# A gated recurrence with a rational MLP on one core: three more accumulating DMAs, two copies moved from ScalarE to VectorE, and all 861 steps in a new order

## The chip, the cores and the metric

The kernel runs on one core of one Trainium2 chip. The metric is device time in microseconds of one execution. Of the kernel before, three runs are shown: 217.76, 218.05 and 218.08 us, median 218.05.

## What is computed

The reference, cut to what matters: a recurrence with a gate per key channel, whose output feeds an MLP with a rational activation.

```
f = 1 / (1 + exp(-f_logit))                        # (4, 8, 768, 48): batch, heads, steps, channels
for t in range(S):
    state = f[t][:, None] * state + outer(k[t], v[t])
    y[t]  = q[t] @ state
x  = y, heads side by side                          # (3072, 384)
h  = x @ w_in                                       # (3072, 2048)
P  = a0 + a1*h + a2*h^2 + a3*h^3
Q  = 1 + |b0|*|h| + |b1|*h^2
out = (P / (Q + 1e-6)) @ w_out                      # (3072, 384)
```

## The kernel before

The work is cut into 12 units of 256 tokens: unit n is chunk n // 4 of batch n % 4, so a unit needs the state that unit n - 4 left. Within a unit a partition holds two neighbouring tokens, and the hidden layer of 2048 lies as 16 blocks (`m`) of 128; the elementwise work on it goes by halves (`0 8`, `8 16`) or quarters (`0 4` and so on).

Nothing orders the steps but a string of 861 steps written out by hand, `ORDER` (lines 19 to 104). Each step issues its instructions on one engine, each engine takes its own in the order of the string, and semaphores hold a step until what it reads is there and what it overwrites has been read. `@s` names the one of four PSUM slots that a step opens; opening it waits for the readers of what lay there. `s` sends a copy to ScalarE (ACT), no letter to VectorE (DVE). The steps that matter here, with their lines in the kernel before:

- `ld` (L200): loads of f, k, q over SP's queue, of v over POOL's; three buffers each, so that a load waits for the last reader of an older one. `wi` (L206) and `wo` (L212) load the two weights over POOL's queue.
- Attention. ACT: `ef` (L278) and `ls` (L283) make log(1 + exp(-f)) of a unit; PE: `cs` (L293) sums it along the tokens; ACT: `A` (L309) takes exp of plus and minus the sum; DVE: `xa` (L315) multiplies A with q (`x` = 0) and k (`x` = 1); PE: `T` (L327) transposes; `Te` (L337 on ACT, L339 on DVE) copies the transposed tile out of PSUM; PE: `sc` (L352); DVE: `mk` (L360) masks; PE: `yi`, `yb` (L374) build y, `kv`, `si` (L421 to L432) the new state; ACT: `ae` (L445), DVE: `st` (L449) close the state; ACT: `ye` (L439) copies y out. POOL: `vm` (L367) packs parts of v.
- MLP. PE: `h` (L458; `ha` and `hb`, L482, for the first block); `hy` (L488) copies h out of PSUM, in quarters; DVE: `sq` (L492) h^2, or ACT: `sa` (L496); DVE: `ab` (L500) |h|.
- The denominator: its sum of h^2 and |h| is made in one of three ways: by PE, `u` (L508), read by `ln` (L513); by DVE, `zv` (L518); or by an accumulating DMA of POOL's queue, `zd` (L522), which adds h2 onto z in SBUF. `lz` (L526) takes the log of z, `ex` (L530) the exp of minus that.
- The numerator: DVE: `p1` (L534), `pm` (L548), `p2` (L539); then the sum of both parts is made by DVE, `tv` (L556), or by an accumulating DMA, `ta` (L552), which adds hy onto g; DVE: `gm` (L560) multiplies by the reciprocal.
- PE: `o` (L570) multiplies with w_out; `oe` (L577) copies out; `so` (L583) stores, on SP's queue but for the last, which is on ACT's. `dz` (L302) are matmuls whose result nobody reads.

A half of `tv` and a half of `ta` write the same bytes; so do halves of `zv` and `zd`. POOL takes its `vm`, its loads and its accumulating DMAs in one line: whichever waits holds up those behind it. The same holds for SP's loads and stores.

Of the kernel before, what the change touches and what calls it, by code (L numbers as in the profile page):

```python
# [13 lines left out]
ALU = mybir.AluOpType  # L14
# [5 lines left out]
ld 0 f 2 4; cz 0; ab_ b a; cu 0; cz 1; ld 0 f 0 2; ld 1 f; ci; cu 1; ld 0 v; ld 0 k 0 2; ld 0 k 2 4; fa  # L20
ld 0 q 2 4; ef 0 2 4; ls 0 2 4; cm; ef 0 0 2; dz 9 @2; cs 0 2 4 @2; fr; cz 3; ls 0 0 2; ld 0 q 0 2; ab_ a s
ld 1 k; dz 5 @3; cs 0 0 2 @3; ef 1; ld 1 q; ls 1; vm 0 1; A 0 1 0 2; wi 12 16 >ls.1; dz 4 @0; cs 1 @0
A 0 1 2 4; xa 0 1 0 2; A 0 0 2 4; wi 8 12; cz 2; A 0 0 0 2; xa 0 1 2 4; dz 3 @1; kv 0 @2; wi 4 8
xa 0 0 0 2; si 0 0; ae 0; dz 1 @1; T 0 0 2 @1; wi 0 4; xa 0 0 2 4; st 0 0; Te 0 0 2 s; T 0 2 4 @3; A 1 1
ld 1 v; Te 0 2 4; A 1 0; vm 0 0; sc 0 0 @1; si 0 1; mk 0 0; sc 0 1 @3; mk 0 1; ld 2 f >mk.0.1; ld 2 k
ld 3 f; yi 0 1 @0; yb 0 0 2; ye 0 0 1 s; xa 1 1; dz 2 @1; yb 0 2 4; ye 0 1 3 s; st 0 1; dz 1 @3
ha 0 12 16 @3; hb 0 12 16; xa 1 0; fb; hy 0 12 16; h 0 8 12 @1; sq 0 12 16; T 1 @3; hy 0 8 12; ab 0 12 16
u 0 12 16 @2; Te 1 s; sq 0 8 12; h 0 4 8 @1; p1 0 8 16; ln 0 12 16; ld 4 f; ab 0 8 12; pm 0 8 16
u 0 8 12 @2; hy 0 4 8; p2 0 8 16; ln 0 8 12; dz 1 @3; sc 1 1 @1; sc 1 0 @3; sq 0 4 8; h 0 0 4 @0; ef 2
ab 0 4 8; mk 1 1; ld 2 q; ls 2; u 0 4 8 @2; hy 0 0 4; mk 1 0; cs 2 @1; ld 3 q; vm 1 1; ln 0 4 8; vm 1 0  # L30
ld 2 v; kv 1 @0; p1 0 0 8; si 1 0; sq 0 0 4; A 2 1; ld 4 q; ld 3 v; ae 1; yb 1 2 4 @2; ab 0 0 4; A 2 0
yb 1 0 2; st 1 0; ld 4 v; xa 2 1; ef 3; yi 1 1; ld 3 k; u 0 0 4 @1; ye 1 s; tv 0 8 16; wo 8 12; si 1 1
ex 0 8 16; h 1 12 16 @2; p2 0 0 8; pm 0 0 8; h 1 0 4 @3; ld 4 k; ln 0 0 4; st 1 1; hy 1 12 16; tv 0 0 8
hy 1 0 4; h 1 4 8 @1; vm 2 1; xa 2 0; wo 12 16; h 1 8 12 @2; hy 1 4 8; ld 5 f; gm 0 8 16; vm 3 1; vm 2 0
wo 0 4; ls 3; T 2 @3; ab 1 0 8; hy 1 8 12; kv 2 @1; sq 1 0 8; Te 2 s; cs 3 @0; vm 3 0; wo 4 8; sq 1 8 16
ld 5 q; si 2 0; ae 2; A 3 0; sc 2 0 @2; sc 2 1 @3; A 3 1; ab 1 8 16; ex 0 0 8; st 2 0; u 1 4 8 @0; mk 2 1
si 2 1; mk 2 0; u 1 0 4 @3; ef 4; ln 1 4 8; st 2 1; yi 2 1 @2; yb 2 0 2; yb 2 2 4; p1 1 0 16; ld 5 k
ln 1 0 4; u 1 8 12 @0; vm 4 0; ld 5 v; ye 2 s; gm 0 0 8; u 1 12 16 @3; ln 1 8 12; xa 3 1; h 2 4 8 @1
ln 1 12 16; pm 1 8 16; ex 1 0 8; h 2 8 12 @3; xa 3 0; h 2 0 4 @0; pm 1 0 8; hy 2 8 12; ld 6 f; hy 2 4 8
p2 1 0 16; kv 3 @2; si 3 0; ae 3; hy 2 0 4; h 2 12 16 @1; st 3 0; tv 1 0 8; sa 2 8 12; T 3 @0; hy 2 12 16  # L40
ab 2 0 8; si 3 1; sq 2 0 8; Te 3 s; ld 6 k; sa 2 12 16; ab 2 8 16; sc 3 1 @3; u 2 4 8 @0; st 3 1; ls 4
# [72 lines left out]
def kernel(  # L114
# [12 lines left out]
    nc = tc.nc  # L127
    B, H, S, D = q.shape
    C = 128
# [4 lines left out]
    KD = DM // P  # L134
# [332 lines left out]
    def fl(t, m0, m1):  # L467
        return t[:, m0:m1, :].rearrange("p m t -> p (m t)")
# [17 lines left out]
    def hy(n, m0, m1):  # L486
        s = unit(n)
        nc.scalar.copy(fl(big(s, "hy", "hy", 3), m0, m1), fl(s["hp", m0], 0, m1 - m0))  # L488
# [140 lines left out]
```

## Time and profile before

| | before |
|---|---|
| median of three runs | 218.05 us |
| span of the profiled execution | 216.3 us |
| instructions in it | 7159 |
| PE, DVE, ACT, POOL busy | 203.2, 202.7, 200.8, 81.6 us |
| moved by DMA | 42.13 MB |

The profiled execution's own time is known by its span alone, from its first to its last instruction; the median stands 1.75 us above that span, and what is worked out below is worked out for the span and carried over with that difference kept. Back to back, instructions of one engine overlap a little in these records, so the cost of one in a busy stretch is the distance from its start to the start of the next, which is less than its duration.

### The profile page before, as it was taken

To read this page: it belongs to the slowest core of one execution; us is meant where nothing else is said; L and a number is where in the kernel's file an instruction comes from. 1 tells how busy PE (TensorE), PEld (TensorE's weight loads), DVE (VectorE), ACT (ScalarE), POOL (GpSimd) and SP (SyncE) were. 2 spreads that over 40 slices of the span, in tenths; PEclk is the share of its full clock that TensorE was granted. 3 is DMA by queue.
4 is the path that set the end of the run, shared out by engine and by line. 5 is a ranking of instruction groups with operands and counts; after the bars stand their busy time and mean duration, and the time that the engine had idled before them with its cause. 6 is when DMAs were issued, how large, how long until landed. Compare 5 with 4: busy or idle time off the path is not lost.

```text
span 216.3 us, 7159 instructions
## 1 busy us (share of the span) xinstructions
PE 203.2 (94%) x3166; PEld 140.1 (65%) x3166; DVE 202.7 (94%) x246; ACT 200.8 (93%) x211; POOL 81.6 (38%) x91
## 2 busy tenths in 40 slices
PE   6989989699799999999999999999999999999993
PEld 2457658468377657658758658668668678676551
DVE  3588999999999999999999999999999999999991
ACT  4746899999999999999999999999999999999991
POOL 5250247120157803014954205954232516433300
PEclk9999999999999999999999999999999999999999
DMA  5999999999598999958999997999889793999863
GB/s 132 248 226 194 243 212 226 207 221 250 136 246 143 231 237 271 149 101 195 197 232 216 211 251 179 173 234 222 160 159 228 142 162 70 170 194 188 154 234 145
DMA packets 60910, 42.13 MB, mean 195 GB/s; under 512 B 51152, under 2 KB 54992, under 8 KB 60880
## 3 DMA queue, kind: packets, MB, share of 16 engines
q0 software_dynamic: 21232, 22.81, 66.0%
q1 hardware_dynamic: 39360, 18.68, 33.7%
q8 instruction: 24, 0.39, 0.7%
q10 hardware_dynamic: 288, 0.20, 0.3%
q14 instruction: 6, 0.05, 0.1%
HBM read 25.17 MB, written 4.72 MB: 138 GB/s over the span
## 4 chain that ended last, share of the span: by engine, by line
ACT 42%; DVE 21%; PE 18%; DMA 8%; issue 6%; POOL 3%; POOLq 0%; ACTq 0%; DVEq 0%
ACT qi L530 11%; ACT hy L488 10%; PE op L570 9%; ACT lq L526 8%; DMA fn<-in_f_logit_dram 4%; DMA z<-h 4%; PE warm L302 3%; DVE gall L548 3%; ACT A L309 3%; DVE scm L360 3%; DVE qkp L315 3%; PE hp L458 2%; DVE gall L560 2%; DVE gall L556 2%; ACT qkT L337 2%
## 5 line engine op out<-in xcount | busy, mean ns | idle before, releaser
L570 PE MATMUL op<-w_out_sb,gall 128*128 128x384 bf16 x384 | 70.1, 326 | 0.4 <-ACT hy L488 0.4
L458 PE MATMUL hp<-xT,w_in_sb 128*128 128x256 bf16 x564 | 65.3, 272 | 1.3 <-ACT xT L439 1.1
L458 PEld LDWEIGHTS <-w_in_sb 128*128 128x128 bf16 x564 | 55.0, 98 | 11.0 <-issue 2.8
L570 PEld LDWEIGHTS <-gall 128*128 128x128 bf16 x384 | 35.5, 98 | 23.6 <-DVE gall L560 0.9
L488 ACT CAST hy<-hp 128x1024 bf16<-128x1024 f32 x48 | 47.4, 1073 | 1.7 <-PE hp L482 1.2
L530 ACT ACTIVATE qi<-lq 128x2048 bf16<-128x2048 f32 (+1 forms) x26 | 46.9, 1845 | 0.0
L367 POOL COPY vmp<-vn 128x128 bf16<-128x128 bf16 x24 | 33.7, 1417 | 32.1 <-DMA vn<-in_v_dram 18.9
L526 ACT ACTIVATE lq<-z 128x2048 f32<-128x2048 bf16 (+1 forms) x20 | 36.9, 1846 | 0.6 <-DMA z<-h 0.5
L552 POOL DMA_DIRECT2D gall<-hy x17 | 14.8, 926 | 50.7 <-ACT A L309 11.5
L522 POOL DMA_DIRECT2D z<-h x18 | 17.3, 1065 | 36.3 <-issue 10.5
L560 DVE TENSOR_TENSOR gall<-gall,qi 128x2048 bf16<-128x2048 bf16 (+1 forms) x26 | 29.6, 1143 | 0.3 <-ACT qi L530 0.2
L548 DVE TENSOR_TENSOR gall<-gall,h 128x2048 bf16<-128x2048 bf16 (+1 forms) x26 | 29.4, 1138 | 0.0
L492 DVE TENSOR_TENSOR h<-hy 128x2048 bf16<-128x2048 bf16 (+1 forms) x26 | 27.3, 1059 | 1.5 <-ACT hy L488 1.4
L360 DVE TENSOR_TENSOR scm<-sc,mask 128x1024 bf16<-128x1024 f32 x24 | 28.4, 1211 | 0.0
L309 ACT ACTIVATE A<-cs 128x768 f32<-128x768 f32 (+1 forms) x26 | 19.6, 816 | 0.0
L500 DVE TENSOR_SCALAR z<-hy 128x2048 uint16<-128x2048 uint16 (+1 forms) x28 | 17.1, 618 | 0.1
L534 DVE TENSOR_SCALAR gall<-hy,a_sb 128x4096 bf16<-128x4096 bf16 (+1 forms) x14 | 16.9, 1210 | 0.2 <-ACT hy L488 0.2
L539 DVE TENSOR_SCALAR hy<-hy,a_sb 128x4096 bf16<-128x4096 bf16 (+1 forms) x14 | 16.6, 1184 | 0.0
L200 POOL DMA_DIRECT2D vn<-in_v_dram x12 | 13.2, 1104 | 2.2 <-PE y L374 2.2
L315 DVE TENSOR_TENSOR qkp<-kn,A 128x768 bf16<-128x768 f32 (+1 forms) x13 | 11.5, 887 | 2.0 <-ACT A L309 2.0
L278 ACT ACTIVATE fn<-fn 128x768 f32<-128x768 f32 (+1 forms) x13 | 10.7, 825 | 2.8 <-DMA fn<-in_f_logit_dram 2.7
L337 ACT COPY qkT<-tp 128x1024 f32<-128x1024 f32 (+1 forms) x12 | 12.5, 1041 | 0.7 <-PE tp L327 0.7
(72 smaller groups left out, 262.2 us busy)
## 6 DMA issues: line engine op xcount, KB each, us to landing
gall<-hy POOLq DMA_DIRECT2D x16, 512.0 KB, 6.7
z<-h POOLq DMA_DIRECT2D x15, 512.0 KB, 7.4
fn<-in_f_logit_dram SPq DMA_DIRECT2D x11, 384.0 KB, 7.4
kn<-in_k_dram SPq DMA_DIRECT2D x11, 384.0 KB, 9.8
qn<-in_q_dram SPq DMA_DIRECT2D x11, 384.0 KB, 7.2
out_dram<-osb SPq DMA_DIRECT2D x11, 384.0 KB, 4.1
vn<-in_v_dram POOLq DMA_DIRECT2D x12, 192.0 KB, 8.0
w_in_sb<-in_moe_w_in_dram POOLq DMA_DIRECT2D x4, 384.0 KB, 8.2
```

Source lines behind the costliest of these rows:

```text
L309: nc.scalar.activation(t, src, AF.Exp, scale=1.0 if x else -1.0)
L315: return nc.vector.tensor_mul(s["qk"][:, :, x, hh, 0:D], s["qk"[x]][:, hh].rearrange("p h i d -> p i h d"), A_sb[:, :, x].rearrange("p i ( ...
L360: return nc.vector.tensor_mul(t, s["sc", g].rearrange("s r a i t -> s (r a) (i t)"), mb)
L367: nc.gpsimd.tensor_copy(s["vm"][:, :, :, 32 * x:32 * x + 16], src)
L458: nc.tensor.matmul(t[:, m - m0, :], w_in_sb[:, kk, m * P:(m + 1) * P], s["x"][:, kk].rearrange("p i j t -> p (i j t)"), start=(kk == 0), s ...
L488: nc.scalar.copy(fl(big(s, "hy", "hy", 3), m0, m1), fl(s["hp", m0], 0, m1 - m0))
L492: return nc.vector.tensor_mul(fl(big(s, "h2", "h2", 2), m0, m1), fl(s["hy"], m0, m1), fl(s["hy"], m0, m1))
L526: nc.scalar.activation(fl(lq, m0, m1), fl(s["z"], m0, m1), AF.Ln, scale=regs[2], bias=1.0 + 1e-6)
L530: nc.scalar.activation(fl(qi, m0, m1), fl(lq, m0, m1), AF.Exp, scale=-1.0)
L548: return nc.vector.tensor_mul(fl(s["g"], m0, m1), fl(s["g"], m0, m1), fl(s["h2"], m0, m1))
L560: return nc.vector.tensor_mul(fl(s["g"], m0, m1), fl(s["g"], m0, m1), fl(qi, m0, m1))
L570: nc.tensor.matmul(s["op", j][:, j, 0:DM], s["g"][:, m, P * j:P * j + P], w_out_sb[:, m, :], start=(s["on", j] == 1), stop=(s["on", j] == KF))
```

## The change

Counted as a set, 13 steps leave the string and 13 come in; the other 848 are the same steps, but nearly all stand at another place.

- Five halves of the numerator's sum go from DVE (`tv`) to an accumulating DMA (`ta`): `0 8 16`, `1 0 8`, `1 8 16`, `2 8 16`, `3 8 16`. Two come back from DMA to DVE: `2 0 8`, `3 0 8`. In unit 11 two quarters change places: `4 8` goes to DMA, `0 4` to DVE.
- One half of the denominator's sum goes from DVE to DMA (`4 8 16`), another comes back (`3 8 16`).
- Two copies out of PSUM go from ACT to DVE: `Te 0 0 2` and `hy 1 0 4`.

So DVE loses three `tv` halves and gains two copies, ACT loses two copies, POOL issues three more accumulating DMAs of 512 KB, and PE has the same instructions in another order. Code for it: `hy` and `ye` take an engine letter (no step gives `ye` the letter `v`).

```
-        k0, k1 = [x for x in args if x != "s"] or (0, KD)
+        k0, k1 = [x for x in args if x not in ("s", "v")] or (0, KD)
...
+        if "v" in args:
+            return nc.vector.tensor_scalar(dst, src, sig[:, 0:1], None, op0=ALU.mult)
+        return nc.scalar.mul(dst, src, regs[0])
...
-    def hy(n, m0, m1):
-        s = unit(n)
-        nc.scalar.copy(fl(big(s, "hy", "hy", 3), m0, m1), fl(s["hp", m0], 0, m1 - m0))
+    def hy(n, m0, m1, eng="s"):
+        s = unit(n)
+        (nc.scalar.copy if eng == "s" else nc.vector.tensor_copy)(
+            fl(big(s, "hy", "hy", 3), m0, m1), fl(s["hp", m0], 0, m1 - m0))
```

Of the string, the parts that the prediction speaks of. The first loads on SP's queue, and the first instructions of ACT:

```
-ld 0 f 2 4; ...; ld 0 f 0 2; ld 1 f; ...; ld 0 k 0 2; ld 0 k 2 4; ...; ld 0 q 2 4; ...; ld 0 q 0 2; ...; ld 1 k; ...; ld 1 q
-ef 0 2 4; ls 0 2 4; ...; ef 0 0 2; ...; fr; ...; ls 0 0 2; ...; ef 1; ...; ls 1; ...; vm 0 1; ...; wi 12 16 >ls.1
+ld 0 f 2 4; ...; ld 1 f; ld 0 f 0 2; ...; ld 0 k 2 4; ld 0 k 0 2; ...; ld 0 q 0 2; ld 0 q 2 4; ...; ld 1 q; ld 1 k
+ef 0 2 4; ls 0 2 4; ...; ef 1; ...; ef 0 0 2; ls 0 0 2; ls 1; ...; wi 12 16 >ls.1; ...; fr
```

ACT around the load of unit 2's f, which is held until `mk 0 1` is done:

```
-ln 0 12 16; hy 0 4 8; ln 0 8 12; ef 2; ls 2
+ln 0 12 16; hy 0 4 8; ef 2; ln 0 8 12; ls 2
```

SP's queue behind that load:

```
-2 f, 2 k, 3 f, 4 f, 2 q, 3 q, 4 q, 3 k, 4 k, 5 f
+2 f, 4 f, 3 f, 2 q, 2 k, 4 k, 3 k, 3 q, 5 q, 4 q, 5 f
```

POOL's queue in the stretch of the weight loads and the first accumulating DMAs:

```
-ld 4 v, wo 8 12, vm 2 1, wo 12 16, vm 3 1, vm 2 0, wo 0 4, vm 3 0, wo 4 8, vm 4 0, ld 5 v, zd 2 8 16
+vm 3 0, ld 4 v, wo 4 8, wo 12 16, ta 0 8 16, vm 2 1, vm 2 0, wo 8 12, wo 0 4, vm 4 1, ta 1 0 8, ta 1 8 16, vm 3 1, zd 2 8 16
```

ACT from the last reader of unit 6's f buffer to `ef 9`, whose load waits for that buffer:

```
-ls 6; lz 3 0 8; ye 4; lz 3 8 16; ef 7; oe 1; Te 5; hy 4 8 12; hy 4 12 16; sa 4 0 4; hy 4 0 4; hy 4 4 8; sa 4 4 8; ae 5; ex 3 8 16; ex 3 0 8; ls 7; ef 9
+ls 6; ex 2 8 16; Te 5; ye 4; lz 3 0 8; oe 1; hy 4 12 16; ef 9
```

Ahead of `ye 5` ACT no longer has `ex 3 8 16`, `ls 7`, `oe 2`, `sa 4 4 8` (nor the two copies that went to DVE), and PE no longer has `cs 6` and 16 of the `o` matmuls of unit 2; these come behind it. Behind `ye 11` each engine has the same steps as before.

More of the change, by code (lines that the diff above doesn't have):

```diff
@@ L25 @@
[L25 to L29, printed above, removed]
@@ new lines @@
+yb 1 2 4; st 1 0; A 2 0; p1 0 0 8; yi 1 1; u 0 0 4 @3; ye 1 s; pm 0 0 8; dz 1 @0; ef 3; si 1 1; h 1 0 4 @0
+xa 2 0; ln 0 0 4; st 1 1; ex 0 8 16; h 1 4 8 @1; ld 5 q; p2 0 0 8; ld 4 q; ld 5 f; hy 1 0 4 v; vm 3 0
+h 1 12 16 @2; ld 4 v; hy 1 4 8; xa 2 1; wo 4 8; h 1 8 12 @0; ls 3; wo 12 16; tv 0 0 8; hy 1 12 16; ld 6 f
+ta 0 8 16; cs 3 @1; ld 5 k; sq 1 0 8; hy 1 8 12; T 2 @2; A 3 0; sq 1 8 16; kv 2 @0; Te 2 s; ab 1 8 16; vm 2 1
+ae 2; A 3 1; sc 2 0 @2; ab 1 0 8; sc 2 1 @3; ex 0 0 8; si 2 0; mk 2 1; vm 2 0; u 1 4 8 @1; wo 8 12; wo 0 4
@@ new lines @@
+ab 3 8 16; o 1 1 0 4 @0; xa 5 1; dz 1 @1; oe 0 0 2 s; sc 4 0 @1; kv 4 @2; lz 2 8 16; mk 4 0; o 1 1 8 12
+sc 4 1 @3; xa 5 0; o 1 0 8 12; ae 4; ex 2 0 8; mk 4 1; o 1 0 12 16; vm 5 0; vm 5 1; si 4 0; ta 2 8 16
+yb 4 0 2 @1; tv 2 0 8; yb 4 2 4; ls 6; o 1 1 4 8; ld 7 v; st 4 0; ex 2 8 16; T 5 @3; ld 9 f; p1 3 0 16
+so 0 0 2 s; si 4 1; ld 8 k; yi 4 1; ld 6 k; yi 4 0; o 1 0 0 4; ld 7 q; pm 3 0 8; Te 5 s; ld 6 q; o 1 1 12 16
+ld 8 q; ye 4 s; st 4 1; sc 5 0 @3; pm 3 8 16; lz 3 0 8; o 1 0 4 8; dz 1 @2; h 4 12 16 @1; zv 3 8 16; oe 1 0 2 s
@@ new lines @@
+vm 8 1; ye 6 s; vm 8 0; xa 7 0; o 3 1 4 8; zd 5 8 16; A 7 1; h 6 4 8 @2; pm 5 0 8; ld 10 q; ex 4 8 16
+so 1 0 2 s; ld 9 q; xa 7 1; h 6 0 4 @0; ld 10 f; pm 5 8 16; ls 8; o 3 0 0 4; hy 6 0 4; ld 11 f; gm 4 0 8
+h 6 12 16 @3; oe 3 0 2 s; gm 4 8 16; hy 6 4 8; h 6 8 12 @0; hy 6 12 16; sq 6 0 8; T 7 @2; hy 6 8 12; p2 5 0 16
+o 4 1 8 12 @1; Te 7 s; o 4 1 12 16; p1 6 0 16; lz 5 0 8; ta 5 0 8; sc 7 0 @0; kv 7 @3; ld 9 v; o 4 0 4 8
+ab 6 0 8; o 4 0 0 4; ta 5 8 16; lz 5 8 16; zv 6 0 8; sc 7 1 @2; o 4 0 8 12; ab 6 8 16; si 7 0; o 4 0 12 16
@@ new lines @@
+pm 11 0 4; o 10 1 8 12; zd 11 12 16; lz 11 0 4; so 7 0 2 s; p1 11 8 16; o 10 1 0 4; lz 11 8 12; tv 11 0 4
+o 10 1 12 16; p2 11 8 16; o 10 1 4 8; ex 11 4 8; pm 11 8 12; o 10 0 12 16; ex 11 0 4; gm 11 4 8; o 10 0 8 12
+tv 11 8 12; ex 11 8 12; o 11 0 4 8 @0; gm 11 0 4; o 11 1 4 8 @3; lz 11 12 16; pm 11 12 16; o 11 0 0 4
+gm 11 8 12; o 11 1 0 4; ex 11 12 16; tv 11 12 16; o 11 0 8 12; oe 10 0 2 s; gm 11 12 16; o 11 1 8 12
+so 10 0 2 s; o 11 0 12 16; o 11 1 12 16; oe 11 0 1 v; so 11 0 1 s; oe 11 1 2 s; so 11 1 2 a
@@ L438, in ye @@
             s["x"] = at.tile([P, KD, 2, UB, R], BF16, name="xT", bufs=2)
[L439 to L440 removed]
+        dst = s["x"][:, k0:k1].rearrange("p k i j t -> p j (k i) t")
+        src = s["y"][:, :, k0 * C:k1 * C].rearrange("p j (k t) -> p j k t", t=R)
+        if "v" in args:
+            return nc.vector.tensor_scalar(dst, src, sig[:, 0:1], None, op0=ALU.mult)
+        return nc.scalar.mul(dst, src, regs[0])
     def ae(n):
```

143 lines of the change are left out of this document (61 added, 82 removed).

## The prediction

> **What bounds the kernel now.** First the page's busy times, then the same by stage.
>
> ```profile
> span 216.3 us, 7159 instructions
> ...
> PE 203.2 (94%) x3166; PEld 140.1 (65%) x3166; DVE 202.7 (94%) x246; ACT 200.8 (93%) x211; POOL 81.6 (38%) x91
> ```
>
> No engine stands out: three are busy over 93% of the span. Where are the missing 6%? The table of windows (columns: stretch, its length, then busy time and count of PE, weight loads, DVE, ACT, POOL, granted clock, DMA share, GB/s) tells it.
>
> ```profile
> 0.00:30.00 30.00, 26.57 (x421) 15.96 (x421) 22.08 (x55) 20.19 (x30) 9.97 (x24) 1.00 1.16 211
> 30.00:100.00 70.00, 65.75 (x1055) 46.21 (x1056) 69.65 (x72) 69.39 (x75) 22.95 (x22) 1.00 1.07 202
> 100.00:190.00 90.00, 88.29 (x1543) 63.71 (x1542) 89.41 (x91) 89.57 (x88) 43.61 (x39) 1.00 0.98 187
> 190.00:212.00 22.00, 21.83 (x148) 13.95 (x146) 21.01 (x30) 21.18 (x20) 5.09 (x6) 1.00 0.84 181
> ```
>
> In the 160 us from 30 to 190 DVE is idle for 0.94 us (160 - 69.65 - 89.41) and ACT for 1.04; both are full, and the end can come earlier there only by work taken off both. PE is idle for 5.96, 4.25 of it before 100. Before 30 there is a head of waits (DVE idle 7.9, ACT 9.8). The granted clock is 1.00 throughout, so no term of the sum is for the clock. Last, the chain of waits (start, length, what) for the end:
>
> ```profile
> 190.54 5.40 PE hp L458 x48
> 195.94 4.55 PE op L570 x28
> 200.49 0.94 PE u L508 x4
> 201.43 11.38 PE op L570 x68
> ```
>
> From the last `ye` on, PE runs from 190.54 to 212.81, 22.3 us without a gap, and a copy and a store follow. The new order leaves PE the same steps behind `ye 11`, so the end moves as `ye 11` moves, and `ye 11` is an ACT step in ACT's full stretch.
>
> **The change part by part.** The costs, from the chain, the groups by form, and the timeline of ACT:
>
> ```profile
> 52.85 1.13 DVE gall L556
> ```
>
> ```profile
> L360 DVE TENSOR_TENSOR scm<-sc,mask 128x1024 bf16<-128x1024 f32 x24 | 28.4, 1211 | 0.0
> L339 DVE COPY qkT<-tp 128x1024 bf16<-128x1024 bf16 x1 | 0.7, 691 | 0.7 <-ACT qkT L337 0.7
> ```
>
> ```profile
> 75.43 2.06 ACT L530 ACTIVATE qi<-lq 128x2048 bf16<-128x2048 f32 x1
> 77.24 0.98 ACT L283 ACTIVATE lsp<-fn 128x768 bf16<-128x768 f32 x1
> 78.20 1.91 ACT L526 ACTIVATE lq<-z 128x2048 f32<-128x2048 bf16 x1
> 80.02 0.79 ACT L439 ACTIVATE xT<-y 128x768 bf16<-128x768 f32 x1
> ...
> 83.85 0.78 ACT L577 COPY osb<-op 128x768 f32<-128x768 f32 x1
> 84.53 1.02 ACT L337 COPY qkT<-tp 128x1024 f32<-128x1024 f32 x1
> 85.43 1.94 ACT L488 CAST hy<-hp 128x1024 bf16<-128x1024 f32 x2
> 87.24 1.06 ACT L496 ACTIVATE h<-hp 128x1024 bf16<-128x1024 f32 x1
> ```
>
> *DVE.* Three `tv` halves go for good: 3 x 1.13 = 3.4 us. `hy 1 0 4` comes: a copy of 128x1024 f32 from PSUM, which DVE does nowhere before. Its nearest rows are the mask (same size and PSUM source, but a second operand, 1.21) and the copy of the transposed tile (as many elements, bf16, 0.69); I take 1.2, since the f32 source is what it shares with the mask. `Te 0 0 2` comes at 0.69, as L339 copies the other half. The quarters of unit 11 and the exchanged denominator halves cancel. DVE: -3.4 + 1.2 + 0.7 = -1.5 (to -2.0 with `hy` at its low end).
>
> *ACT.* `hy 1 0 4` goes: two `hy` last from 85.43 to 87.24, so one is 0.9. `Te 0 0 2` goes too, but it stands in the head, where ACT is idle for 9.8 us and next waits for a load; I cost it at nothing. ACT: -0.9.
>
> *PE* keeps its work. Its cover is those 5.96 us of idle. The rest of its reordering I cost at nothing: the idle time is the bound of what it could win or lose.
>
> *POOL and DMA.* Three accumulating DMAs more. POOL's issuing has room (38% busy). The data do not go through a free resource:
>
> ```profile
> gall<-hy POOLq DMA_DIRECT2D x16, 512.0 KB, 6.7
> ...
> fn<-in_f_logit_dram SPq DMA_DIRECT2D x11, 384.0 KB, 7.4
> ```
>
> Of the three net halves two are of unit 1 and one of unit 0. `ta 0 8 16` is issued behind `wo 12 16`, and in POOL's line `vm 2 1`, `vm 2 0` and two weight loads stand behind it, for all of which their readers come later than a landing of 6.7 would; I cost it at nothing, and its upper end is the rival on DMA.
>
> *The head.* ACT's rows round unit 2's f, and what the load competes with:
>
> ```profile
> 16.06 9.14 DMA fn<-in_f_logit_dram
> ```
>
> ```profile
> 7.76 0.84 ACT L283 ACTIVATE lsp<-fn 128x768 bf16<-128x768 f32 x1
> ...
> 9.67 3.04 POOL L206 DMA_DIRECT2D w_in_sb<-in_moe_w_in_dram  x4
> ...
> 10.92 1.03 DVE L315 TENSOR_TENSOR qkp<-qn,A 128x384 bf16<-128x384 f32 x2 [0.51 <-DMA qn<-in_q_dram]
> ```
>
> ```profile
> 23.78 1.03 ACT L513 ACTIVATE lq<-u 128x1024 f32<-128x1024 f32 x1
> 25.22 0.84 ACT L278 ACTIVATE fn<-fn 128x768 f32<-128x768 f32 x1 [0.41 <-DMA fn<-in_f_logit_dram]
> 26.10 0.84 ACT L283 ACTIVATE lsp<-fn 128x768 bf16<-128x768 f32 x1
> ```
>
> The load is held until `mk 0 1`, is issued at 16.06 and lands 9.14 later, at 25.20, behind the weight loads; ACT waits 0.41 for it. The new order asks for it one `ln` earlier: `ef 2`, then `ln 0 8 12` (0.9, from 23.78 to the end at 24.81 less overlap). Ahead of it, `wi 12 16` no longer stands behind a `vm`, so the weights start just behind `ls 1` (its end stood at 8.60, so some 8.7 and not 9.67) and are through up to 0.9 earlier. The masks start about 0.3 earlier, since q's halves are now loaded in the order in which DVE takes them (0.51 of waiting before). So the load lands 0.3 to 0.9 earlier: 24.6 by the middle. Then `ef 2` to 25.35, `ln` to 26.25, and `ls 2` starts there: 0.15 later than the 26.10 of before. Bounds: -0.15 (landing at 24.3) to +0.75 (at 25.2).
>
> *A new tight place.* `ld 9 f` waits for `ls 6`, and `ef 9` now stands only six ACT steps behind it. By the rows above: `ex` 1.81 (75.43 to 77.24), `Te` 0.90, `ye` 0.7 to 0.8, `lz` 1.82, `oe` 0.68, `hy` 0.9: 6.8 us of room. That very load was issued at 78.25 before, and the answer for its tile in that window reads:
>
> ```profile
> DMA to landing us min/median/max: 6.1/6.1/6.1
> ```
>
> 6.1 fits into 6.8, with 0.7 to spare: nothing. What is queued behind `ef 9` if it is late is all of ACT.
>
> **Sum**, for the span: ACT -0.9, head +0.15, `ef 9` 0, PE 0: -0.75. DVE has -1.5 and is no longer what ACT waits for. 216.3 - 0.75 = 215.55, and with the 1.75 that the median stands above the span, **217.3 us**. Its own range is 216.7 to 217.9: the head's bounds are -0.15 and +0.75, and `ef 9` may add its first tenths.
>
> **The rivals.**
>
> *A, more than forecast.* With DVE relieved by 1.5, the 1.04 us that ACT was idle between 30 and 190 go as well: -0.75 - 1.0, 216.3. Against it: these waits were for PE and for a landing (`ef 9` adds one of the latter), and PE is as full as before.
>
> *B, PE takes over.* Ahead of `ye 5` ACT sheds `ex`, `ls`, `oe`, a square and the copy that went: 1.81 + 0.96 + 0.68 + 0.9 + 0.9 = 5.25 us (the square taken as long as a `hy`), PE only 16 `op` matmuls (11.38 / 68 = 0.167 each) and a `cs` of four as wide, 3.3 together. So PE has to come 2 us sooner there than its own work allows, out of 4.25 us idle between 30 and 100. If that idle is not to be had, ACT and DVE wait up to 2 us; half of it eats the gain: 218.3 at most, 217.9 to 218.3, no change.
>
> *C, slower: the adds and the loads share one path.* The place is ACT's `ef`. The answer for SP's and POOL's loads between 15 and 60 reads:
>
> ```profile
> DMA to landing us min/median/max: 6.0/8.5/16.2
> ```
>
> There, with weights and loads in flight, a landing takes 8.5 by the median and not 7.4. The change puts `ta` transfers into just that time and behind it. `ef 5`: its load is the one of 16.2, issued at 35.34 and landing at 51.5; one load more (`5 q`, 0.39 MB) and `ta 0 8 16` (0.52 MB) now go ahead, 0.92 MB / 202 GB/s = 4.5 us.
>
> ```profile
> 35.34 4.65 SPq L200 DMA_DIRECT2D fn<-in_f_logit_dram  x1
> ...
> 57.28 0.88 ACT L278 ACTIVATE fn<-fn 128x768 f32<-128x768 f32 x1
> ```
>
> Its reader started at 57.28, 5.7 later; it now comes 1.6 us earlier in ACT's line (`hy 1 0 4` and `ls 4` no longer ahead): 4.5 + 1.6 - 5.7 = 0.4 late, unless the two weight loads that moved behind give their place. `ef 9`: with 8.5 instead of 6.1, 1.7 late. `ef 2` at its bound, +0.6. Together -0.75 + 0.4 + 1.7 + 0.6 = +1.95: **220.0**; with `ef 9` and half of the rest, 219.5. It decides from a landing of `9 f` above 7.5, where the gain is gone. For it: 16.2 is a fact of this kernel, and the adds are added to it. Against: the load of `9 f` itself took 6.1.
>
> The Trainium skill, DMA: Bandwidth & Descriptors, section Issuing engines are not separate DMA queues, says that DMAs issued from ScalarE, SyncE or GpSimd end up on the same 16 DMA engines and interleave. By that rule a sum moved from DVE to POOL's queue is paid for by SP's loads, as C has it; by a queue of POOL's own it would cost them nothing and the forecast would stand. The trace leans to the rule (8.5 beside 7.4), and that is why C has the chance that it has.
>
> **How the numbers follow.** Forecast 0.38, A 0.10, B 0.17, C 0.35. A measurement of this kernel can tell about 0.2% from no change: 0.44 us, 217.6 to 218.5. Most of the forecast (0.34) and A are faster: 0.44. B's larger part (0.12) and the forecast's upper end (0.04): 0.16 within. C and what of B goes past 218.5: 0.40 slower. The likeliest is 217.3. The range goes from A, 216.2, to the middle of C, 219.4, and leaves out C's upper half and A's far end, some 0.2. It holds both signs; the forecast's own range is 216.7 to 217.9.
>
> **What would show it.** Right: ACT idle about 1 us between 30 and 190, as before; `ef 2` starting at 24.5 to 24.9 with a wait of up to 1 us behind a DMA; no wait at `ef 5` and `ef 9`; DVE idle 1 us more than before in the full stretch; PE running 22.3 us without a gap from the last `ye`. A: ACT idle under 0.5 us. B: ACT and DVE waiting for PE (`hp`, `y`, `tp`) between 60 and 120, PE idle under 2 us before 100. C: `fn` at L278 waiting for DMA by over a microsecond in all, or `lq` and `gall` waiting for `z` and `gall` landings. What makes the prediction wrong without any of these: `hy` on DVE well over 1.2, or a gap in PE's last 22 us.

## The result and the profile after

The changed kernel is slower: median 221.96 us (221.32 to 222.91, four runs) against 218.06 (217.76 to 218.11), ratio 1.0162, 95% interval 1.0125 to 1.0199. The forecast of 217.3 had the wrong sign, and its range (to 219.4) doesn't hold the time. (Here and below, runs in a slower state, over 1.5% above the fastest of their kernel, are left out of the ratios.)

The page of the changed kernel, first its busy times:

```profile
span 219.8 us, 7156 instructions
...
PE 202.2 (92%) x3159; PEld 139.9 (64%) x3166; DVE 201.9 (92%) x245; ACT 199.3 (91%) x209; POOL 79.6 (36%) x94
```

ACT has 1.5 us less than before: the 0.9 of the prediction, and 0.6 for `Te 0 0 2` in the head, which it had costed at nothing. DVE has 0.8 less, where the prediction had 1.5. The windows of the changed kernel, with the columns as before:

```profile
0.00:30.00 30.00, 24.24 (x352) 14.74 (x354) 21.66 (x54) 18.19 (x27) 10.53 (x24) 1.00 1.13 210
30.00:100.00 70.00, 67.92 (x1132) 48.52 (x1135) 69.25 (x73) 69.75 (x77) 24.29 (x29) 1.00 1.15 209
100.00:190.00 90.00, 87.09 (x1528) 62.06 (x1526) 89.09 (x90) 89.42 (x87) 38.51 (x36) 1.00 1.01 200
190.00:212.00 22.00, 20.66 (x141) 13.61 (x141) 20.62 (x29) 19.50 (x18) 6.27 (x7) 1.00 0.84 181
```

From 30 to 190 ACT and DVE are nearly as full as before (idle 0.83 and 1.66 us; before 1.04 and 0.94). From 190 to 212 nothing is full any more: PE is idle for 1.34 where it was idle for 0.17. The chain of waits tells why; before, its last 22 us were PE and nothing else, now they are two landings (start, length, what):

```profile
189.82 6.22 DMA z<-h
...
197.95 0.99 ACT hy L487
198.93 1.82 ACT qi L530
...
203.26 1.02 POOL gall L552
...
205.09 6.00 DMA z<-h
211.12 1.07 ACT lq L526
...
214.05 1.49 PE op L570 x8
215.56 0.48 ACT osb L577
```

The step times in the timelines cut the 3.47 us between the two spans into four parts. "To `ye 1`" is the end of that copy, "middle" runs from there to the end of `ye 11`, "tail" to the end of PE's last matmul, "end" to the end of the span.

| profile | to `ye 1` | middle | tail | end | span |
|---|---|---|---|---|---|
| before | 31.67 | 158.82 | 22.30 | 3.50 | 216.29 |
| after | 32.47 | 158.15 | 24.90 | 4.24 | 219.76 |
| difference | +0.80 | -0.67 | **+2.60** | +0.74 | +3.47 |

In this profile the middle gains somewhat less than was forecast (0.9), and the tail, which the forecast carried over as it was, loses four times that.

### The profile page after: what moved, and what is told of

The parts are those of the page before. It is cut to its first block, busy times and chain, and to the rows that moved or that the text cites. A ratio compares the mean times of both kernels' runs of the same rounds, so it can differ in the third digit from the quotient of the medians.

```text
span 219.8 us, 7156 instructions
## 1 busy us (share of the span) xinstructions
PE 202.2 (92%) x3159; PEld 139.9 (64%) x3166; DVE 201.9 (92%) x245; ACT 199.3 (91%) x209; POOL 79.6 (36%) x94
## 4 chain that ended last, share of the span: by engine, by line
ACT 37%; PE 19%; DMA 15%; DVE 14%; issue 11%; POOL 2%; ACTq 0%; SPq 0%; POOLq 0%
ACT hy L487 10%; DMA z<-h 9%; ACT qi L530 7%; DMA fn<-in_f_logit_dram 7%; PE op L570 7%; PE hp L457 5%; ACT lq L526 4%; DVE scm L356 3%; ACT A L305 3%; ACT lq L513 2%; ACT qkT L333 2%; ACT fn L274 2%; ACT lsp L279 2%; DVE gall L548 2%; ACT xT L439 2%
## 5 line engine op out<-in xcount | busy, mean ns | idle before, releaser
L522 POOL DMA_DIRECT2D z<-h x18 | 19.3, 1072 | 54.4 <-DVE z L500 19.8
L363 POOL COPY vmp<-vn 128x128 bf16<-128x128 bf16 x24 | 27.3, 1166 | 29.3 <-DMA vn<-in_v_dram 20.8
L552 POOL DMA_DIRECT2D gall<-hy x20 | 18.9, 976 | 35.8 <-ACT lq L526 11.2
L356 DVE TENSOR_TENSOR scm<-sc,mask 128x1024 bf16<-128x1024 f32 x24 | 28.9, 1216 | 0.3 <-PE sc L348 0.2
L305 ACT ACTIVATE A<-cs 128x768 f32<-128x768 f32 (+1 forms) x26 | 20.1, 823 | 0.6 <-PE cs L289 0.5
L274 ACT ACTIVATE fn<-fn 128x768 f32<-128x768 f32 (+1 forms) x13 | 11.2, 870 | 4.3 <-DMA fn<-in_f_logit_dram 4.3
L439 ACT ACTIVATE xT<-y 128x768 bf16<-128x768 f32 (+2 forms) x13 | 10.5, 817 | 3.8 <-PE y L370 3.8
L323 PE MATMUL tp<-ident,qkp 128*128 128x128 bf16 x192 | 12.7, 219 | 0.0
## 6 DMA issues: line engine op xcount, KB each, us to landing
fn<-in_f_logit_dram SPq DMA_DIRECT2D x11, 384.0 KB, 10.6
```

What stands on the lines that cost most here:

```text
L305: nc.scalar.activation(t, src, AF.Exp, scale=1.0 if x else -1.0)
L356: return nc.vector.tensor_mul(t, s["sc", g].rearrange("s r a i t -> s (r a) (i t)"), mb)
L363: nc.gpsimd.tensor_copy(s["vm"][:, :, :, 32 * x:32 * x + 16], src)
L522: nc.gpsimd.dma_start(out=fl(s["z"], m0, m1), in_=fl(s["h2"], m0, m1), accum_op=ALU.add)
```

## The experiments

The three parts of the new order can be put together with those of the old one, since the string is cut at `ye 1` and at `ye 11`. The rows of all profiles:

| run | to `ye 1` | middle | tail | end | ratio to before |
|---|---|---|---|---|---|
| e1: old tail | 32.40 | 158.34 | 22.19 | 4.44 | 1.0072 (1.0035 to 1.0109) |
| e2: old head | 31.54 | 157.92 | 23.97 | 4.08 | 1.0077 (1.0041 to 1.0113) |
| e3: old head and tail | 31.79 | 158.31 | 22.19 | 4.42 | 1.0113 (1.0060 to 1.0166) |
| e4: before, new tail | 31.68 | 159.16 | 24.70 | 3.50 | 1.0128 (1.0087 to 1.0169) |
| e5: before, work exchanged | 31.71 | 159.39 | 22.28 | 3.49 | 1.0039 (1.0008 to 1.0070) |
| e6: before, `hy` on DVE | 31.56 | 160.36 | 22.53 | 3.49 | 1.0053 (1.0017 to 1.0089) |
| e7: before, three adds by DMA | 33.00 | 159.15 | 22.33 | 3.49 | 0.9987 (0.9957 to 1.0017) |
| e8: e3, room for loads | 31.37 | 159.06 | 22.19 | 4.04 | 1.0070 (1.0040 to 1.0100) |
| e9: e4, stores early | 33.54 | 158.52 | 22.83 | 3.50 | 1.0028 (0.9999 to 1.0058) |
| e10: e4, `hy` early | 32.82 | 158.80 | 24.43 | 3.49 | 1.0081 (1.0060 to 1.0102) |
| e11: e3, eight copies more | 31.49 | 159.57 | 22.32 | 4.33 | 1.0029 (1.0001 to 1.0057) |
| e12: after once more | 32.58 | 159.72 | 23.83 | 4.39 | one run, 222.49 us |
| e13: e10, `sq` early | 31.76 | 158.88 | 23.46 | 3.50 | 1.0050 (1.0021 to 1.0079) |
| e14: before, load of 2 f early | 32.26 | 158.90 | 22.28 | 3.50 | 1.0000 (0.9979 to 1.0020) |
| e15: e13, stores early too | 32.04 | 158.76 | 22.85 | 3.49 | 1.0023 (0.9993 to 1.0052) |

### Which part loses: e1 to e4

Theory T: the order behind `ye 11` costs it. Rivals: the head (H), or the loads and added transfers of the middle (C). e1 has the steps of the change up to `ye 11` and then the tail of before:

```
-ye 11; lz 10 0 8; ...; hy 11 0 4; ...; lz 10 8 16; ...; hy 11 8 12; ...; h 11 12 16; ex 10 8 16; ...; hy 11 12 16; gm 10 8 16; ...; sq 11 12 16; ...; so 9; so 8; ...; zd 11 12 16; ...; so 7
+ye 11; lz 10 0 8; ...; hy 11 0 4; ...; h 11 12 16; hy 11 8 12; ...; lz 10 8 16; ...; hy 11 12 16; ...; ex 10 8 16; ...; sq 11 12 16; ...; gm 10 8 16; ...; zd 11 12 16; ...; so 9; ...; so 7; ...; so 8
```

> The changed kernel up to ye 11, then all that the kernel before has behind ye 11, in the order of before. Theory T (the loss is made behind ye 11, by the order of the last unit's quarters, and nowhere else by more than 1 us): 2.7 to 3.5 us less than the changed kernel, 218.4 to 219.3. Rival C (the loss comes from the accumulating DMAs beside the loads, before ye 11): no change, 221 to 222.5.

e2 has before's order up to `ye 1` (in the main `ln 0 8 12; ef 2; ls 2` again), the rest as in the change (one PSUM slot, of `h 1 0 4`, renumbered).

> The changed kernel, but its steps up to ye 1 in the order of before (with Te 0 0 2 back on ACT, as before has it). Theory T: the head has lost 0.8 us by ye 1, of which 0.4 stood in the first load already, so 0.4 to 0.8 less than the changed kernel, 221.2 to 221.6. Rival H (the head is where the loss arises, and the end only passes it on): 2 us less or more, under 220.

e3 has both, so that only the middle is new.

> Both of it: only the steps between ye 1 and ye 11 stand in the new order. Theory T: the middle gained 0.7 us in the trace, from ye 1 to ye 11, so 0.3 to 0.9 less than the kernel before, 217.1 to 217.8. Rival C: the middle is where the three added transfers lie, so 219.5 or more.

e4 is before with the tail of the change.

> The kernel before up to ye 11, then the steps behind ye 11 in the order of the changed kernel. Theory T: 2.7 to 3.5 us more than before, 220.7 to 221.5. Rival C or H: as before, 217.8 to 218.5.

T holds for the tail: it goes with its order, 22.19 in e1 and e3, 24.70 in e4; taking the old order back is worth 2.7 in e1, and the new one costs before 2.4 in e4, whose time, 220.75, is in T's range (e1's, 219.55, is just above it). T does not hold for the rest. e2 took 219.8 in three runs, where H had put it. Its step times show the head for 0.9 of that, at `ye 1`; another 0.9 came in the tail, though its order is that of the change: that one order took 24.90 in the profile of the change, 23.97 in e2 and 23.83 in e12. In the runs the head's part isn't seen: e1 has the new head, e3 the old one, and e3 isn't faster. And e3, new in the middle alone, missed: 1.0113, some 2.5 us slower than before, is where C had put it, though its profile shows a middle 0.51 shorter; its other runs took more than the profiled one. Two things are seen behind it. The column "end" is 0.5 to 0.95 longer in every kernel with the new middle; and the profiled middle isn't the usual one (below, e11 and e12).

### What the work is worth without the order: e5 to e7

e5 exchanges the work (`hy 1 0 4` to DVE, the adds of `0 8 16`, `1 0 8`, `1 8 16` to DMA, the other halves swapped) in the order of before, only the `gm` that now wait for a landing standing later:

```
-tv 0 8 16; ...; hy 1 0 4; ...; tv 1 0 8; ...; tv 1 8 16; ...; ta 2 0 8; ...; tv 2 8 16
+ta 0 8 16; ...; hy 1 0 4 v; ...; ta 1 0 8; ta 1 8 16; ...; ta 2 8 16; ...; tv 2 0 8
```

> The order of before, with only the work exchanged: hy 1 0 4 on DVE, the halves 0 8 16, 1 0 8 and 1 8 16 added by DMA in place of DVE, the other exchanged denominator halves as in the change; no step moves but the three gm that now wait for a landing. The tail and the head are those of before. Theory W (in the middle the end follows the work that ACT and DVE are given; ACT sheds 0.9, DVE 2.2): 217.4, 0.5 to 1.0 under before. Rival C (each added accumulating transfer slows the loads, and the fs of units 4 to 6 come late): 0.5 to 2 above before. Rival P (PE is what ACT and DVE wait for there): within 0.3 of before.

e6 is the first half of that, e7 the second:

```
-hy 1 0 4
+hy 1 0 4 v
```

> Before with one edit: the copy hy 1 0 4 (128x1024 f32 from PSUM) goes from ACT to DVE. ACT sheds 0.9, DVE takes 1.22. If ACT alone sets the pace of the middle (as the prediction had it): 0.9 less, 217.3. If DVE is bound just as tightly: 0.3 to 1.2 more, 218.5 to 219.4. If PE sets it: within 0.3 of before.

```
-tv 0 8 16; ...; tv 1 0 8; ...; tv 1 8 16
+ta 0 8 16; ...; ta 1 0 8; ta 1 8 16
```

> Before with one edit: the three sums 0 8 16, 1 0 8 and 1 8 16 go from DVE (1.13 us each) to accumulating DMAs, and their three gm stand a few steps later in DVE's order. If ACT alone sets the pace: within 0.3 of before. If DVE is bound as tightly: up to 1.0 less. Rival C (the transfers slow the loads): 0.5 to 2 more, with ACT waiting for fn behind a DMA.

The stretch from `ye 1` to `ye 2`, where the copy and the first of the three sums lie, in the windows of before, e6 and e7 (the stretch, its length, then PE, weight loads, DVE, ACT):

```profile
31.67:46.28 14.61, 12.80 (x231) 9.26 (x231) 14.61 (x17) 14.61 (x17) 6.28 (x10) 1.00 1.32 213
```

```profile
31.56:47.30 15.74, 12.91 (x231) 9.31 (x232) 15.74 (x18) 14.15 (x16) 5.41 (x8) 1.00 1.34 208
```

```profile
33.00:47.60 14.60, 13.31 (x233) 9.57 (x234) 13.11 (x15) 14.60 (x18) 6.46 (x11) 1.00 1.31 206
```

In before both engines are busy for all of the 14.61 us. With the copy moved, DVE stays full and the stretch is 1.13 longer, while ACT idles; with the adds taken away, ACT stays full, the stretch is as long as it was, and DVE idles for 1.49. Two engines are bound at once here: work taken off DVE alone is worth nothing, and work put on it costs nearly its full length, in the runs too (e6 is 1.2 us slower, e7 as before). e5 takes work off both and gains nothing either: it is 0.8 us slower, which is where its rival C had put it. In the old order the relieved engines wait, ACT for PE and DVE for ACT. Its longest waits from `ye 1` to `ye 11`, of ACT and of DVE (us in total, times, longest):

```profile
ACT hy L485 <- PE hp L455: 0.7, 1, 0.7
```

```profile
DVE z L498 <- ACT hy L485: 1.5, 2, 1.1
```

Another 0.5 us of ACT is a wait for the f of unit 6, and 0.8 of DVE one for a k; before has neither. e7 shows where the former comes from. The median landing of an f, first in e6 (the copy alone), then in e7 (the adds alone), and ACT's wait for it in e7 between `ye 1` and `ye 11`:

```profile
fn<-in_f_logit_dram SPq DMA_DIRECT2D x11, 384.0 KB, 6.9
```

```profile
fn<-in_f_logit_dram SPq DMA_DIRECT2D x11, 384.0 KB, 10.4
```

```profile
ACT fn L272 <- DMA fn<-in_f_logit_dram: 0.6, 1, 0.6
```

The fs of units 7 and 8 took 6.4 and 6.9 us in before and in e6, 15.6 and 13.5 in e7, 15.2 and 13.3 in e5. So the three added transfers do slow the loads, as C has it; in the old order nearly all of that falls into the time ahead of their use (9.9 us and more are left for units 7 and 8).

So the 0.5 to 0.9 that the new middle gains in its better profiles needs the new order; the exchange alone costs 0.6 in its profile.

### Where the tail loses it: e9, e10, e13, e15

The last quarter of the denominator, `zd 11 12 16`, is issued 12.6 us behind `ye 11` in before and 14.5 behind it in the change, and lands in 3.25 and 6.0. Its reader is `lz 11 12 16`. Its issue and its reader, in before and then after:

```profile
203.12 0.85 POOL L522 DMA_DIRECT2D z<-h  x1 [1.60 <-DVE h L492]
208.36 1.09 ACT L526 ACTIVATE lq<-z 128x1024 f32<-128x1024 bf16 x1
```

```profile
205.09 1.16 POOL L522 DMA_DIRECT2D z<-h  x1 [0.81 <-DVE h L492]
211.12 1.06 ACT L526 ACTIVATE lq<-z 128x1024 f32<-128x1024 bf16 x1 [1.32 <-DMA z<-h]
```

In before it lands at 206.37, 2.0 us ahead of its reader; in the change the reader waits for it. Part of the later issue is order (e10 and e13 below), part is a wait. The new order puts `lz 10 8 16` ahead of `hy 11 8 12` on ACT, and in the profile of the change ACT waits 1.19 us there for `zd 10 8 16` (the first landing of the chain above); in e2 and e12, with the same tail, that wait is 0.17 and 0.12, `zd 11 12 16` is issued only 0.8 later than in before, and the tail is 1.5 to 1.7 longer and not 2.6. The DMA view of 203 to 206 us, before and then after (count, KB each, median us to landing):

```profile
out_dram<-osb SPq DMA_DIRECT2D x3, 384.0 KB, 4.0
z<-h POOLq DMA_DIRECT2D x1, 256.0 KB, 3.2
```

```profile
out_dram<-osb SPq DMA_DIRECT2D x3, 384.0 KB, 4.2
...
z<-h POOLq DMA_DIRECT2D x1, 256.0 KB, 6.0
```

In before the three stores are issued behind it, in the change ahead of it. e9 takes two of them away from there:

```
-oe 8; ...; so 9; so 8; ...; zd 11 12 16; ...; so 7
+oe 8; so 7; so 8; ...; so 9; ...; zd 11 12 16
```

> As e4 (the order of before up to ye 11, then the new tail), with one edit: the stores so 7 and so 8 are issued right behind oe 8, some 10 us earlier, so that only so 9 is in flight beside zd 11 12 16. In e4 that transfer of 256 KB took 6.43 us beside the three stores, in before 3.25 with no store ahead of it. If the stores are the half of the tail's loss that stands in the landing: it lands in 4.0 to 4.7, PE's end comes 1.7 to 2.4 earlier (213.1 to 213.8), time 218.4 to 219.1. Rival (the landing is slow for another reason, or the loss is all in the later issue): landing still 6, time as e4, 220.7.

```profile
out_dram<-osb SPq DMA_DIRECT2D x1, 384.0 KB, 3.6
...
z<-h POOLq DMA_DIRECT2D x1, 256.0 KB, 4.2
```

As expected: 4.2, and the tail is 22.83, 1.9 shorter than in e4 (PE's end, 214.90, is above the expected one because this profile's head came 1.9 late). No wait for z is left there: it lands 0.4 ahead of its reader. e10 instead mends the order of PE and ACT, and e13 that of DVE as well:

```
-h 11 8 12; ...; h 11 12 16; ex 10 8 16; ...; hy 11 12 16
+h 11 8 12; h 11 12 16; ...; hy 11 12 16; ex 10 8 16
```

> As e4, with one edit: h 11 12 16 stands right behind h 11 8 12 on TensorE, and hy 11 12 16 ahead of ex 10 8 16 on ACT, as in before; the stores stay. If the later issue is the other half of the tail's loss: sq and zd 11 12 16 come some 1.8 earlier, thus ahead of the stores too, landing 3.3 to 4.5, PE's end 212.8 to 213.8, time 218.1 to 219.1. Rival (lz 10 8 16 ahead of hy 11 8 12 alone costs it): under 0.5 gained, 220.3 to 220.7.

```
-gm 10 8 16; ...; ab 11 12 16; ...; sq 11 12 16
+ab 11 12 16; sq 11 12 16; gm 10 8 16
```

> As e10, with ab 11 12 16 and sq 11 12 16 ahead of gm 10 8 16 in DVE's order, as in before; the stores stay as in the new tail. In e10 hy 11 12 16 came 1.9 earlier, but sq waited in DVE's line behind gm 10 8 16, which waited 0.76 for ex 10 8 16. If the order of ACT and DVE is what delays zd 11 12 16: it is issued some 2 us earlier (12.5 behind ye 11 and not 14.6), ahead of the stores, lands in 3.3 to 4.2, and PE ends 22.3 to 22.9 behind ye 11 and not 24.4; time 218.3 to 219.0. Rival (only the landing beside the stores counts): PE's end over 23.8 behind ye 11, time 220.

e10 missed: the tail is 24.43, 0.3 shorter, and the time, 220.2, is all but the rival's. Its timeline of DVE shows the reason: `hy 11 12 16` had ended at 201.95, but ahead of `ab` (L497) and `sq` (L489) DVE waits at `gm 10 8 16` for the very `ex 10 8 16` that was put behind it.

```profile
203.79 1.23 DVE L557 TENSOR_TENSOR gall<-gall,qi 128x2048 bf16<-128x2048 bf16 x1 [0.76 <-ACT qi L527]
204.93 0.42 DVE L497 TENSOR_SCALAR z<-hy 128x1024 uint16<-128x1024 uint16 x1
205.27 0.68 DVE L489 TENSOR_TENSOR h<-hy 128x1024 bf16<-128x1024 bf16 x1
```

In e13, with a tail of 23.46 between the two expectations, the transfer is issued at 12.7 behind `ye 11`, as expected, but it didn't land in 3.3 to 4.2:

```profile
out_dram<-osb SPq DMA_DIRECT2D x3, 384.0 KB, 6.0
...
z<-h POOLq DMA_DIRECT2D x1, 256.0 KB, 6.3
```

POOL takes 1.0 us to issue it, and the stores are issued 0.2 behind its start, so they are in flight together; in before they came 1.6 behind it. Being first in time by a hair isn't enough. e15 does both:

> As e13 (new tail with hy, ab and sq 11 12 16 early), and so 7 and so 8 issued right behind oe 8, as in e9. If landing and order are all of the tail's loss: zd 11 12 16 lands in 3.3 to 4.2 of its issue, no wait for z is left ahead of the last lz, and PE ends 22.2 to 22.6 behind ye 11 (22.30 in before, 22.83 in e9, 23.46 in e13); time 217.9 to 218.7. Rival (a third part, in PE's order of the last o matmuls): PE's end 22.8 or more behind ye 11, with a gap in PE ahead of o 10 or o 11.

`zd 11 12 16` took 5.0 to landing, more than expected, but it landed 0.7 ahead of its reader. The tail is 22.85, no shorter than with the stores alone. So the gains don't add: both edits shorten one and the same wait for z, and none of it is left in e9 or e15. Of the 2.4 us of e4 against before, some 1.9 are that wait, and the 0.5 left are the rival's third part, a gap of PE ahead of the `o` of unit 10: in e9 PE waits 0.36 for `hy 11 12 16`, in e15 0.44 for `gm 10 8 16`, which `o 10 1 8 12` now needs earlier. PE in e15:

```profile
204.37 9.28 PE L567 MATMUL op<-w_out_sb,gall 128*128 128x384 bf16 x56 [0.44 <-DVE gall L557]
```

### The head: e14

```
-mk 0 0; ...; mk 0 1; ld 2 f >mk.0.1
+mk 0 0; ld 2 f >mk.0.0; ...; mk 0 1
```

> Before with one edit: ld 2 f is held behind mk 0 0 and not mk 0 1, and so is issued some 1.2 us earlier. In before ACT waits 0.41 for it at ef 2, and in other profiles with the same head ef 2 started between 24.9 and 27.1. If the landing of unit 2's f sets the end: it lands 0.5 to 1.2 earlier, the wait of 0.41 goes, the time is 0.4 to 0.8 less (217.6 to 218.0) and spreads less. Rival (the load then takes the transfer time of the weights, and h 0 12 16 or hy 0 8 12 come later): no change or up to 0.8 more.

The runs don't differ from before, which is where the rival had put them; whether its reason holds isn't shown. Issued at 14.86 instead of 16.06, the load landed 0.6 later in this profile (10.9 us instead of 9.14), and PE waits for weights:

```profile
PEld L451 <- DMA w_in_sb<-in_moe_w_in_dram: 0.9, 1, 0.9
PE hp L451 <- DMA w_in_sb<-in_moe_w_in_dram: 0.6, 1, 0.6
PEld L475 <- DMA w_in_sb<-in_moe_w_in_dram: 0.6, 1, 0.6
```

`ls 2` comes 0.6 later and PE's end 0.65 later: in this profile the head passes to the end whole. But here the first weights were issued at 10.33, 0.7 us later than in before, and that was ahead of the edited load. e7 has the head of before unedited and its first weights at 10.41; it shows the first two of these waits just as long, and the load landing at 26.38, later than the 25.79 of e14. Late weights go with a late landing in all profiles with the unedited old head: 24.9 to 25.6 in the ten whose first weights were issued between 9.4 and 9.8, 26.3 to 27.1 in the three (e7, e9, e10) with 10.1 to 10.8.

### Why the runs of the new middle spread: e8, e11, e12

Theory F: the new middle leaves little time between a landing and its use, so that an execution with slower transfers stalls. e8 gives room to three loads that in e3 landed 0.10 to 1.33 us ahead of use:

```
-ld 4 q; ...; ld 5 f; ...; ef 5; ls 4; ls 5; ...; ef 7; ...; ef 9; ...; ls 7; ...; ls 9
+ld 5 f; ld 4 q; ...; ls 4; ef 5; ls 5; ...; ef 7; ls 7; ...; ef 9; ls 9
```

> The new middle between the old head and the old tail (as e3), with room given to three loads: ld 5 f is issued ahead of ld 4 q, and ef 5, ef 7 and ef 9 stand just ahead of their ls 5, ls 7 and ls 9. In the profile of e3 these three landed 0.10, 1.00 and 1.33 us ahead of their use (5.7, 19.2 and 10.9 in before). Theory F (the new middle has little room left behind its landings, so executions with somewhat slower transfers stall, which spreads the times of e1 to e3 and puts their median above their profiled one): the spread falls to under 1 us and the median comes to 217.3 to 217.8, under before. Rival (the spread has another cause, such as the sums' own landings zd and ta): spread and median as e3, 219 to 220.

e12 is the changed kernel again, e11 is e3 with eight tiny copies on ACT in the head, meant for the column "end":

> The changed kernel once more, for a second profile: where two executions of the same order differ. In the runs so far it took 221.32 to 222.91. If the difference between executions stands in the landing of unit 2's f (e7's profile had it 1.2 later than before's, with the same head), the step times differ by one amount from ls 2 on; if it stands in the close landings of the middle (theory F), they part further on, at an ef, lz or gm that waits for a DMA.

> As e3 (the new middle between the old head and the old tail), with eight copies of 128x1 added on ACT between 2.1 and 4.4 us, where it waits for the first load. In the profiles the last store took 2.40 to 2.83 in all five kernels with the new middle and 1.88 to 1.90 in all five with the old one; in the former an instruction fetch (the queue named q14) falls 1.0 to 1.3 us behind ACT's issue of that store, in the latter 5 to 6 us ahead of it. Theory I (the fetch is ACT's, stands at a fixed place of its instruction stream, and shares a DMA engine with the store): eight more instructions bring the fetch 4 to 8 us earlier, the last store takes 1.9, the span is 0.5 to 0.9 under e3's, 215.8 to 216.2. Rival (the fetch is another engine's, or the store is slow for another reason): the last store stays at 2.4 to 2.8 and the span at 216.5 to 217. The eight copies cost nothing, or up to 0.3 in the head.

e8 missed: 218.35 to 220.87, a spread of 2.5 us, little less than e3's 3.0 (218.91 to 221.89), and a median of 220.0. Nor is such a spread the new middle's own: beside e8, before took 217.40 to 220.27 in 34 runs, and e9, with the old middle, 218.44 to 221.68. What sets the new middle apart is the median. But e12 caught a stall in the act. Up to `ye 3` its steps are 0.1 behind those of the first profile of the same order; then the load of unit 7's f takes 12.1 us where it took 10.0, and ACT's timeline, first of after, then of e12, reads:

```profile
68.94 1.03 ACT L274 ACTIVATE fn<-fn 128x768 f32<-128x768 f32 x1
```

```profile
70.68 0.84 ACT L274 ACTIVATE fn<-fn 128x768 f32<-128x768 f32 x1 [1.34 <-DMA fn<-in_f_logit_dram]
```

`ye 4` is 1.5 later, and the `ye` behind it 1.3 to 1.8. (In before this load landed 19 us ahead of its use.) e11, whose middle is that of e3, lost 1.26 in it, with waits of the same kind:

```profile
ACT fn L279 <- DMA fn<-in_f_logit_dram: 1.2, 2, 0.7
ACT lq L531 <- DMA z<-h: 1.0, 2, 0.8
```

So the new middle is 157.92 to 159.72 long in seven profiles (after, e1 to e3, e8, e11, e12), the old one 158.52 to 159.16 in seven (before, e4, e9, e10, e13 to e15): shorter at best, longer when a load is late. That such stalls happen is shown; that they are all of the spread is not, since e8 took three of the places away and kept it. How far the spread reaches shows in e3 and e11, one order but for the eight copies: 1.0113 and 1.0029. By none of its ratios was the new middle faster than before.

The column "end" stands apart from the stalls. The last store, 192 KB, takes 1.9 us with the old middle. The DMA views of the end, of before and then of e3 (for the queue: count, MB, share of 16 engines):

```profile
out_dram<-osb ACTq DMA_DIRECT2D x1, 192.0 KB, 1.9
```

```profile
q14 instruction: 1, 0.01, 0.6%
...
out_dram<-osb ACTq DMA_DIRECT2D x1, 192.0 KB, 2.8
```

In all seven profiles of the new middle a fetch of instructions on queue q14 falls beside this store, which then takes 2.4 to 2.8; in the old middle's it lies 5 us or more ahead of the store, or none shows in the last 15 us. e11 tried to move it by lengthening ACT's stream: it stayed (store 2.72, end 4.33), so that theory fell. Whose fetch it is, and why the middle's order places it, stays open; that it is the fetch that slows the store fits 7 of 7 and was not forced by an experiment.

## Why the prediction was wrong

- **"The new order leaves PE the same steps behind `ye 11`, so the end moves as `ye 11` moves."** This is the step that failed. `ye 11` moved by 0.13, PE's end by 2.73. As many steps, yes (one `o` block and one quarter of a sum are others), but not in the same order on PE, ACT, DVE and SP's queue, and the 22.3 us of PE without a gap were taken for a property of the work, where they hung on `zd 11 12 16` landing 2.0 us ahead of its reader. The change spent that slack: issue 1.85 later against `ye 11`, landing 2.75 longer, less the 2.0 there were: 2.6. e9 shows that the landing is slow beside the stores and that the wait for it is 1.9 of the 2.4 us of e4. The prediction named "a gap in PE's last 22 us" as what would refute it, and didn't work it out, though the order of the tail lay open to be compared.
- **Head, +0.15 (bounds to +0.75).** +0.80 at `ye 1`. The wrong term is the landing, forecast at 24.6, since the weights were to be through up to 0.9 earlier and the masks 0.3 earlier. The weights were issued at 9.18 and not 8.7, and the last of them landed 0.3 later than in before (22.92 against 22.58); the masks ended 0.2 later (16.24 against 16.03). The load landed at 25.70, 9.43 behind its issue, and ACT waited 1.15 ahead of `ef 2`:

```profile
16.27 9.43 DMA fn<-in_f_logit_dram
```

```profile
25.72 0.84 ACT L274 ACTIVATE fn<-fn 128x768 f32<-128x768 f32 x1 [1.15 <-DMA fn<-in_f_logit_dram]
26.47 1.00 ACT L513 ACTIVATE lq<-u 128x1024 f32<-128x1024 f32 x1
27.38 0.83 ACT L279 ACTIVATE lsp<-fn 128x768 bf16<-128x768 f32 x1
```

  With `ln 0 8 12` now behind `ef 2`, the whole of it is added to `ls 2` (27.38 against 26.10).
- **ACT -0.9.** Near in size in the profiled execution (-0.67 in the middle), but by luck: the seven profiles of the new middle lie between -0.90 and +0.90 of the old one in before. It is wrong in its reason: "DVE has -1.5 and is no longer what ACT waits for" treats ACT as the bound and DVE as free. e6 and e7 show both bound, and e5 shows that the work alone, without the order, gains nothing. In e11 and e12 late landings take the gain back.
- **`hy` on DVE 1.2.** Right:

```profile
L487 DVE CAST hy<-hp 128x1024 bf16<-128x1024 f32 x1 | 1.2, 1218 | 0.0
```

- **`ef 9`, nothing.** Right: its load took 6.0 and it didn't wait; nor did `ef 5`, by 0.4 us.
- **POOL and DMA, nothing.** In the waits of the first profile's middle nearly so. But the median landing of an f went from 7.4 to 10.6 and that of the adds from 6.7 to 7.7; e7 shows that the adds alone bring the f to 10.4 (e5, with the copy too, to 9.2), and it is for such an f that e12 stalls:

```profile
gall<-hy POOLq DMA_DIRECT2D x19, 512.0 KB, 7.7
...
fn<-in_f_logit_dram SPq DMA_DIRECT2D x11, 384.0 KB, 10.6
```

- **Rival C** has the sign and its mechanism (added transfers slow the loads; e7 shows it), but not the place: in the middle ACT waits at `ef 7` and not at `ef 5` and `ef 9`, and that in the second profile alone (in e11 at `ef 7` and `ef 9`); and the tail, the largest part, it didn't name. **B** (PE takes over) didn't happen: PE has 0.3 us more of busy time between `ye 1` and `ye 11` and is waited for by no more than tenths. **A** fell with the tail.
- By what the Trainium skill says in DMA: Bandwidth & Descriptors, section Issuing engines are not separate DMA queues, transfers issued by different engines interleave on the same 16 DMA engines. The trace agrees at the tail: the 256 KB from POOL took 3.2 us ahead of SP's stores, 4.2 and 5.0 beside one (e9, e15), and 5.4 to 6.4 beside three (e10, after, e13, e4). The prediction cited it for the loads of the middle and didn't apply it to the stores.

## What to carry to other kernels

An engine that runs without a gap to the end bounds the end only for the order in which it was seen: before carrying such a stretch over to a new order, look up how much slack the landings in it had, and recount it with every queue that changed. Where two engines are both full, look for what takes work off both: here work taken off one alone was worth nothing, and work put on one cost nearly its full length. A stretch can be shorter in one profile and its kernel slower by the median; what an order leaves between a landing and its first reader has to be read beside the stretch's length.

## What the runs showed of the hardware that was not expected

- Three more accumulating DMAs of 512 KB took the loads of two later fs from 6.4 and 6.9 us to 15.6 and 13.5 (before and e7), with no change in the time of the kernel.
- A transfer that is issued 0.2 us ahead of three stores landed no sooner than one issued behind them: 6.3 us (e13) and 6.0 (after); issued 1.6 ahead it took 3.25 (before).
- With one and the same order up to there, the load of unit 2's f landed between 24.9 and 27.1 us in the profiles with the old head, late where the weights ahead of it were issued late, and the end moved with it.
- A fetch of instructions beside a store of 192 KB goes with 2.4 to 2.8 us to landing instead of 1.9, in seven profiles of seven.
